# Issuing the first three up-weight loads from GpSimd's queue instead of SyncE's

## The chip, the cores and the metric

The kernel runs on one core of a Trainium2 chip. The metric is the device time of one execution in microseconds (us); lower is better. Before the change the median of three runs is 611.11 us (610.91 to 612.06).

## The reference

Two blocks run one after the other. The first is a linear attention with decay: 4 batches, 8 heads, 768 tokens, head size 64, worked in blocks of 64 tokens. Each block's output is its own masked scores times its values, plus its queries times a state that is carried from block to block:

```python
intra = einsum('bhic,bhjc->bhij', qb, kb) * Dmask[None]
intra = einsum('bhij,bhjd->bhid', intra, vb)
inter = einsum('bhid,bhde->bhie', qb * lam_pow[None], kv_state)
out[:, :, sl] = intra + inter
kv_state = lam_block * kv_state + einsum('bhsd,bhse->bhde', kb * rev_pow, vb)
```

Its output is laid out as `x`, 3072 tokens by 512 columns, and goes through a feed-forward block with a leaky ReLU:

```python
h = x @ w_in                    # (3072, 512) @ (512, 2048)
g = np.maximum(0.01 * h, h)
return (g @ w_out).astype(np.float32)
```

The weights `w_in` ("up") and `w_out` ("down") come as 64-bit floats, so one number of theirs is 8 bytes in memory.

## The kernel before, in words

**Attention.** The 3072 tokens are 24 chunks of 128 tokens (two blocks of 64 each). For chunk `c`, `load_kq` (L330) loads k and q in two halves of 128 KB each, and `load_v` (L374) loads v as one transfer of 256 KB. There are two buffers for each of k, q and v, used by turns, so that a load of chunk `c` has to wait until chunk `c - 2` has been read. TensorE transposes k and q (`transposes`, L391), ScalarE copies the transposes to SBUF (L402, L403), VectorE or GpSimd multiply in the decays (k at L407, q at L411), TensorE makes the scores and the product of k and v (`scores`, `quad` at L312), VectorE masks the scores (L440) and adds the product to the state (L445, L447), and GpSimd decays the state for the next block (L450). Then TensorE makes the output (L312 again), which ScalarE and VectorE split into three parts `xh`, `xl`, `xm` (L495, L496, L498) for an exact product in a faster number format.

**Up weights.** `w_in` is cut into 8 pairs of 128 columns. `w_in(p)` (L593) handles a pair in two halves `h`. For each half `to_float32` (L544) loads 512 KB of 64-bit floats into one of three `raw` buffers (L554), and turns them into 32-bit floats by three ScalarE instructions (L566, L568, L570) and two VectorE instructions (L572, L573). `parts` (L575) then splits the pair into `wh`, `wl`, `wm` (L579 or L581, L584, L590). The counter `n_raw` numbers these loads, and `raw[n_raw % 3]` is the buffer. The first three loads are both halves of pair 1 and the first half of pair 0.

**Products.** `up` (L616, matmuls at L628) multiplies a group of four chunks with a pair of weights and stores the result in DRAM; `down` (L676, matmuls at L688) reads it back and multiplies it with the down weights.

**Order.** All of this is written into a planner (`Plan`, L37). Each step has an engine and a planned cost; DMAs are on a lane of their own, called "DMA". `emit` runs a list schedule over these costs and issues the instructions in the planned order, so that each engine's queue has a fixed order. The plan also puts in idle transposes (`busy`, L262, L265) that keep TensorE running in gaps it foresees. Loads of q, k, v and weights are all issued from SyncE (SP). In the first 33 us SP's order is: k, q, v of chunks 0 and 1, weights (pair 1, first half), q and k of chunk 2, weights (pair 1, second half), v of chunk 2, q, k of chunk 3, q of chunk 4, v of chunk 3, weights (pair 0, first half), k of chunk 4, and so on.

A load needs its buffer free; beyond that, each DMA issued from SP takes one of eight completion semaphores by turns and waits for the DMA that had it before, eight DMAs earlier.

Of the kernel before, what the change touches and what calls it, by code (L numbers as in the profile page):

```python
# [36 lines left out]
class Plan:  # L37
# [23 lines left out]
    def add(self, eng, us, fn, reads=(), writes=(), rank=0.0):  # L61

        n, deps = len(self.ops), set()
        for k in reads:
            w, r = self.last.setdefault(k, [None, []])
            if w is not None:
                deps.add(w)
            r.append(n)
        for k in writes:
            w, r = self.last.setdefault(k, [None, []])  # L70
            if w is not None:
                deps.add(w)
            deps.update(r)
            self.last[k] = [n, []]
        deps.discard(n)
        ways = {eng: us} if isinstance(eng, str) else dict(zip(eng, us))
        if self.slack:
            self.more[n] = self.slack
        if self.chain is not None:
            self.chains[self.chain].append(n)  # L80
        self.ops.append((ways, fn, deps, (self.rank + rank, n), set(writes)))
# [81 lines left out]
def kernel(  # L163
# [10 lines left out]
    nc = tc.nc  # L174
# [34 lines left out]
    def sb(shape, name, dt=F32):  # L209
        return pool.tile(shape, dt, name=name, tag=name)  # L210
# [13 lines left out]
    raw = [sb([P, 2 * d_model], f"raw{i}") for i in range(NRAW)]  # L224
# [53 lines left out]
    def move(us, fn, reads, writes, issue=0.5, rank=0.0, slack=SLACK):  # L278

        plan.slack = slack if steady else EARLY_SLACK  # L280
        if steady and not rank:
            rank = FIRST
        add("DMA", length(us, issue), fn, reads, writes, rank=rank)
        plan.slack = 0.0
# [257 lines left out]
    n_raw = 0  # L542

    def to_float32(kind, p, h, dst, key, after=()):  # L544

        nonlocal n_raw
        j, n_raw = n_raw % (1 if kind == "wo" else len(raw)), n_raw + 1
        r, low, kl = raw[j], lows[n_raw % 2], f"low{n_raw % 2}"
        d = dst.bitcast(I32)

        def get():
            r64 = r.bitcast(I64)
            if kind == "wi":
                nc.sync.dma_start(out=r64.rearrange("p (k f) -> p k f", k=2),  # L554
                                  in_=w_in_r[:, 2 * h:2 * h + 2, p * 2 * P:(p + 1) * 2 * P])
            else:
                nc.sync.dma_start(out=r64, in_=moe_w_out[(2 * p + h) * P:(2 * p + h + 1) * P, :])

        def words(i, dt):
            return r.bitcast(dt).rearrange("p (n two) -> p n two", two=2)[:, :, i]  # L560

        def addend(dt, i):
            return low.bitcast(dt).rearrange("p (n two) -> p n two", two=2)[:, :, i]

        move(1.6, get, after, [f"raw{j}"])
        add("ACT", 0.67, lambda: nc.scalar.activation(out=dst, in_=words(1, F32), func=AF.Abs, scale=2.0 ** -110),  # L566
            [f"raw{j}"], [key])
        add("ACT", 0.78, lambda: nc.scalar.activation(out=addend(U16, 0), in_=words(0, U32), func=AF.Copy, bias=0.0, scale=2.0 ** -29),  # L568
            [f"raw{j}"], [kl])
        add("ACT", 0.77, lambda: nc.scalar.activation(out=addend(F16, 1), in_=words(1, F32), func=AF.Copy, bias=0.0, scale=2.0 ** -100),  # L570
            [f"raw{j}"], [kl])
        add("DVE", 0.42, lambda: nc.vector.tensor_scalar(d, d, 3, None, op0=ALU.logical_shift_left), [], [key])  # L572
        add("DVE", 1.0, lambda: nc.vector.tensor_tensor(d, d, low, op=ALU.add), [kl], [key])  # L573
# [19 lines left out]
    def w_in(p):  # L593
        for h in range(2):
            to_float32("wi", p, h, w32[:, h, :], f"w32{h}")
        parts(p, w32f, ["w320", "w321"])
# [5 lines left out]
    def w_out(p, h, after):  # L602
        to_float32("wo", p, h, w32[:, h, :], f"w32{h}", after)
        if h == 1:
            move(1.5, lambda: nc.sync.dma_start(out=WO[p], in_=w32f), ["w320", "w321"], [f"WO{p}"])
# [198 lines left out]
```

## Time and profile before

| what | value |
|---|---|
| median of three runs | 611.11 us |
| profiled execution, its own time | 611.72 us |
| its span, first to last instruction | 609.9 us |
| TensorE busy | 598.7 us, 98% of the span |
| VectorE / ScalarE / GpSimd busy | 312.6 / 270.3 / 83.2 us |
| DMA moved | 104.66 MB, mean 172 GB/s |
| granted TensorE clock | 0.999 |

The profile is of one execution. Busy time of an engine leaves out DMA-issuing instructions. In the timeline a line gives the start and the duration in us, the engine, the line of the kernel, what was written from what, how many instructions are merged (x4), and in brackets the idle time before, with what ended it. "SPq" is SP's own queue: the duration is how long SP was taken up with issuing. "Landing" is the time from the start of the issue until the completion was signalled.

### The profile page before, as it was taken

What the parts mean: (1) busy time and instruction counts of PE and PEld (TensorE: products, weight loads), DVE (VectorE), ACT (ScalarE), POOL (GpSimd) and SP (SyncE); (2) the same over time, 40 slices, a digit from 0 to 9 for tenths busy, and PEclk for the clock granted to TensorE, in tenths of its full rate; (3) what the DMA queues carried; (4) which work ended last, traced back from release to release, by engine and by line L of the source; (5) the groups of instructions that cost most, each with busy time, mean ns of one, the idle gap of its engine ahead of it and who ended that gap; (6) DMA issues with size and microseconds to landing.
All of it is one profiled execution on the core that took longest, in us unless ns stands there. A gap on an engine that the chain in (4) does not pass through costs nothing.

```text
span 609.9 us, 12921 instructions
## 1 busy us (share of the span) xinstructions
PE 598.7 (98%) x5402; PEld 496.0 (81%) x5402; DVE 312.6 (51%) x412; ACT 270.3 (44%) x434; POOL 83.2 (14%) x90
## 2 busy tenths in 40 slices
PE   7899999999999999999999999999999999999997
PEld 6678888888878888888888888888888888888886
DVE  5999980254253344335356745545454544635531
ACT  4678874444455656555576522222222313214111
POOL 1654400144142013113000000000000000000000
PEclk9999999999999999999999999999999999999999
DMA  9999976446799879976775943523434343433201
GB/s 211 225 261 257 267 197 163 132 112 158 166 219 267 209 201 244 248 225 182 291 248 207 287 158 103 173 70 139 138 103 133 111 136 108 134 103 124 84 1 69
DMA packets 141162, 104.66 MB, mean 172 GB/s; under 512 B 117040, under 2 KB 117808, under 8 KB 141104
## 3 DMA queue, kind: packets, MB, share of 16 engines
q1 hardware_dynamic: 140960, 103.83, 58.4%
q8 instruction: 42, 0.69, 0.5%
q14 instruction: 16, 0.13, 0.1%
q10 hardware_dynamic: 144, 0.00, 0.0%
HBM read 68.16 MB, written 35.65 MB: 170 GB/s over the span
## 4 chain that ended last, share of the span: by engine, by line
PE 94%; DVE 3%; DMA 1%; ACT 1%; SPq 0%; issue 0%; DVEq 0%
PE b L628 42%; PE b L688 18%; PE po L688 11%; PE psc L688 11%; PE psc L312 4%; PE po L312 4%; PE pt L688 4%; PE pt L391 1%; PE po L391 1%; DMA att<-in_k_dram 1%; DMA raw<-in_k_dram 0%; DVE att L440 0%; DVE att L411 0%; DVE att L447 0%; DVE w L572 0%; DVE wm L590 0%
## 5 line engine op out<-in xcount | busy, mean ns | idle before, releaser
L670 ACT ACTIVATE xh<-att 128x1024 fp32r<-128x1024 f32 x48 | 50.9, 1061 | 147.1 <-PE b L688 145.1
L671 DVE SCALAR_TENSOR_TENSOR xl<-att,xh 128x1024 fp32r<-128x1024 f32 x48 | 58.6, 1222 | 98.5 <-ACT xh L670 98.5
L628 PE MATMUL b<-xh,wh 128*128 128x512 f32 (+1 forms) x392 | 102.9, 386 | 0.8 <-ACT xh L495 0.8
L628 PE MATMUL b<-xm,wm 128*128 128x512 f32 (+1 forms) x392 | 103.2, 391 | 0.0
L628 PE MATMUL b<-xl,wl 128*128 128x512 f32 (+1 forms) x392 | 102.7, 386 | 0.0
L628 PEld LDWEIGHTS b<-xh,wh 128*128 128x128 f32 x392 | 72.6, 188 | 16.4 <-ACT xh L495 0.9
L628 PEld LDWEIGHTS b<-xl,wl 128*128 128x128 f32 x392 | 72.6, 188 | 14.8
L628 PEld LDWEIGHTS b<-xm,wm 128*128 128x128 f32 x392 | 71.2, 188 | 14.7
L649 ACT ACTIVATE gs<-b 128x512 f32<-128x512 f32 x96 | 57.0, 596 | 47.3 <-PE b L628 41.9
L646 ACT ACTIVATE b<-b 128x512 f32<-128x512 f32 x96 | 56.0, 584 | 49.5 <-PE b L628 49.3
L688 PE MATMUL b<-wh,xh 128*128 128x512 f32 x192 | 74.7, 389 | 0.0
L688 PE MATMUL b<-wl,xl 128*128 128x512 f32 x192 | 74.7, 389 | 0.0
L673 DVE SCALAR_TENSOR_TENSOR xm<-xl,xh 128x1024 fp32r<-128x1024 f32 x48 | 58.8, 1225 | 5.2 <-DVE xl L671 0.5
L440 DVE TENSOR_TENSOR att<-psc,att 128x512 f32<-128x512 f32 x24 | 16.5, 687 | 63.6 <-PE psc L312 63.4
L688 PEld LDWEIGHTS b<-wh,xh 128*128 128x128 f32 x192 | 36.1, 188 | 7.5
L688 PEld LDWEIGHTS b<-wl,xl 128*128 128x128 f32 x192 | 36.0, 188 | 7.5
L407 POOL TENSOR_TENSOR att<-att 128x512 f32<-128x512 f32 (+1 forms) x23 | 25.8, 1122 | 98.8 <-PE po L391 54.9
L450 POOL TENSOR_TENSOR att<-att 128x256 f32<-128x256 f32 x40 | 32.8, 821 | 44.5 <-DVE att L447 44.5
L572 DVE TENSOR_SCALAR w<-w 128x512 int32<-128x512 int32 x32 | 17.0, 530 | 40.8 <-ACT w L566 40.8
L688 PE MATMUL psc<-wh,xh 128*128 128x512 f32 x96 | 37.3, 389 | 0.0
L688 PE MATMUL psc<-wl,xl 128*128 128x512 f32 x96 | 37.3, 389 | 0.0
L688 PE MATMUL psc<-wm,xm 128*128 128x512 f32 x96 | 37.3, 389 | 0.0
(73 smaller groups left out, 809.7 us busy)
## 6 DMA issues: line engine op xcount, KB each, us to landing
att<-g SPq DMA_DIRECT2D x48, 512.0 KB, 3.3
g<-gs SPq DMA_DIRECT2D x47, 512.0 KB, 3.8
raw<-in_moe_w_in_dram SPq DMA_DIRECT2D x16, 512.0 KB, 5.7
raw<-in_moe_w_out_dram SPq DMA_DIRECT2D x16, 512.0 KB, 4.6
att<-in_k_dram SPq DMA_DIRECT2D x48, 128.0 KB, 4.3
att<-in_v_dram SPq DMA_DIRECT2D x24, 256.0 KB, 4.6
out_dram<-gs SPq DMA_DIRECT2D x23, 256.0 KB, 2.0
wo<-w SPq DMA_DIRECT2D x8, 512.0 KB, 5.2
```

The source lines that it names most:

```text
L312: nc.tensor.matmul(dst[HALF[cols]], lhsT=lhsT[HALF[rows]], rhs=rhs[HALF[rows]], start=start, stop=True, skip_group_check=True)
L407: lambda e="POOL": ENG[e].tensor_tensor(kr[nr], kr[nr], _bc(pow_k, 3, D)[nr], op=ALU.mult), ["fk"], [f"k{i}"])
L440: add("DVE", 0.69, lambda: nc.vector.tensor_tensor(sc, psc[:, :, lower, :], decay, op=ALU.mult), ["psc", "fk"], ["sc"])
L450: add("POOL", 0.7, lambda new=new, j=j: nc.gpsimd.tensor_tensor(state[(j + 1) % 4], new, _bc(lam_c, 2, D), op=ALU.mult), [f"st{j % 4}", "f ...
L572: add("DVE", 0.42, lambda: nc.vector.tensor_scalar(d, d, 3, None, op0=ALU.logical_shift_left), [], [key])
L628: nc.tensor.matmul(dst, lhsT=w[z][:, kk * 2 * P + f * P:kk * 2 * P + (f + 1) * P], rhs=x[z][:, kk, toks], start=start and kk == 0, stop=kk ...
L646: add("ACT", ns, lambda b=b: nc.scalar.activation(out=b, in_=b, func=AF.Copy, bias=0.0, scale=S + 1.0), [], [kb], rank=-1.5)
L649: add("ACT", ns, lambda b=b, r=r: nc.scalar.activation(out=r, in_=b, func=AF.Prelu, bias=0.0, scale=1.0 / WS, alpha=0.01), [kb], [f"gs{jg} ...
L670: add("ACT", 1.05, lambda: nc.scalar.activation(out=h, in_=graw[j], func=AF.Copy, bias=0.0, scale=NEAR), reads, wr("h"))
L671: add("DVE", 1.25, lambda: nc.vector.scalar_tensor_tensor(l, graw[j], 1.0, h.bitcast(F32), op0=ALU.mult, op1=ALU.subtract), reads + [f"rh{ ...
L673: add("DVE", 1.25, lambda: nc.vector.scalar_tensor_tensor(m, l.bitcast(F32), -S, h.bitcast(F32), op0=ALU.mult, op1=ALU.add), [f"rh{j}", f" ...
L688: nc.tensor.matmul(acc[tb][z // 2][:, cols], lhsT=ring[j][z][:, f * T + tb * P:f * T + (tb + 1) * P], rhs=W[pp][z][:, f * d_model:(f + 1) ...
```

## The change

The first three calls of `to_float32` (those in which `n_raw`, already counted up, is at most the number of `raw` buffers) issue their load from GpSimd's queue. Everything else is as before; the planner sees the same steps with the same costs, so the order on TensorE, VectorE and ScalarE stays as it was, SP's queue loses three entries, and GpSimd's queue gets three.

```diff
@@ -548,10 +548,13 @@
         r, low, kl = raw[j], lows[n_raw % 2], f"low{n_raw % 2}"
         d = dst.bitcast(I32)
 
+        first = n_raw <= len(raw)
+
         def get():
             r64 = r.bitcast(I64)
             if kind == "wi":
-                nc.sync.dma_start(out=r64.rearrange("p (k f) -> p k f", k=2),
+
+                (nc.gpsimd if first else nc.sync).dma_start(out=r64.rearrange("p (k f) -> p k f", k=2),
                                   in_=w_in_r[:, 2 * h:2 * h + 2, p * 2 * P:(p + 1) * 2 * P])
             else:
                 nc.sync.dma_start(out=r64, in_=moe_w_out[(2 * p + h) * P:(2 * p + h + 1) * P, :])
```

On GpSimd's queue the first load stands right after the start-up memsets (L268), ahead of the decay of k of chunk 1 (L407). The second stands right after that L407, ahead of the first decay of the state (L450). The third stands after the fourth L450, ahead of the fifth. None of the three waits for anything but its place in that queue, as the `raw` buffers are still unused.

## Prediction

> **What bounds the kernel now.** I read the page's busy times first, then the windows by stage.
>
> ```profile
> PE 598.7 (98%) x5402; PEld 496.0 (81%) x5402; DVE 312.6 (51%) x412; ACT 270.3 (44%) x434; POOL 83.2 (14%) x90
> ```
>
> ```profile
> 0.00:35.00 35.00, 28.39 (x613) 22.53 (x616) 25.75 (x52) 20.03 (x36) 15.17 (x22) 1.00 0.95 218
> 35.00:70.00 35.00, 35.00 (x550) 29.52 (x543) 32.92 (x44) 28.98 (x54) 16.68 (x13) 1.00 0.89 251
> ```
>
> The columns are the window, its length, then busy us of PE, PEld, DVE, ACT and POOL, the granted clock, the DMA share and GB/s. TensorE is without a gap from 35 us on; its idle time, 6.6 us of the 11.2 in all, lies in the first 35 us, and 3.8 more is the tail after its last matmul. So the change, whose loads all lie in the first 26 us, can only move the point at which TensorE's unbroken run begins. Whatever that start shifts by, the end shifts by. DMA is at 0.95 in the same window: issue slots are not all that is scarce there.
>
> Next, SP's timeline. It issues back to back from 0.74 us to 31 us, so each removed entry brings later ones forward:
>
> ```profile
> 1.78 1.06 SPq L337 DMA_DIRECT2D att<-in_q_dram  x2
> ...
> 6.73 1.12 SPq L554 DMA_DIRECT2D raw<-in_moe_w_in_dram  x1
> ...
> 10.29 1.92 SPq L554 DMA_DIRECT2D raw<-in_moe_w_in_dram  x1
> ...
> 15.19 2.87 SPq L337 DMA_DIRECT2D att<-in_k_dram  x2
> ...
> 19.25 0.46 SPq L376 DMA_DIRECT2D att<-in_v_dram  x1
> 19.75 0.57 SPq L554 DMA_DIRECT2D raw<-in_moe_w_in_dram  x1
> ```
>
> Then TensorE and VectorE where they wait for loads:
>
> ```profile
> 5.50 1.06 PE L391 MATMUL pt<-att 128*128 128x128 f32 x4
> ...
> 23.33 0.44 PE L391 MATMUL pt<-att 128*128 128x128 f32 x2 [0.45 <-DMA att<-in_q_dram]
> ...
> 24.49 1.16 PE L312 MATMUL psc<-att 64*64 64x64 f32 x64 [0.72 <-DVE xl L496]
> ...
> 25.71 0.69 DVE L440 TENSOR_TENSOR att<-psc,att 128x512 f32<-128x512 f32 x1 [1.35 <-PE psc L312]
> ```
>
> ```profile
> att<-in_q_dram SPq DMA_DIRECT2D x1, 128.0 KB, 3.4
> ...
> att<-in_v_dram SPq DMA_DIRECT2D x1, 256.0 KB, 5.1
> ```
>
> The first of these two lines is the second half of q of chunk 0 (issued 2.33 us, so landed at 5.7); the second is v of chunk 3, issued 19.25, landed 24.35. Two load waits sit on the path. The transposes of q of chunk 0 at 5.50 take 1.06 us, against 0.66 for the same four later: they wait for that half, with no slack. And the matmul at 24.49, put down to VectorE, starts right after v of chunk 3 landed; that is the real releaser. VectorE, busy without a real gap from 12.48 to 24.36, idles 1.35 us for it.
>
> **What the Trainium skill says.** "DMA: Bandwidth & Descriptors", section "Issuing engines are not separate DMA queues": DMAs of all issuers run on the same 16 engines, so another issuer saves only sequencer time. Its section "Queues, rings and completion order" adds that an engine goes round robin, a packet at a time, between queue rows that have work; no stretch here shows it, as nearly all bytes are on one queue (q1). Its section "Anatomy of one DMA — SWDGE (gpsimd) path" prices a DMA issued from GpSimd at 2.0 us plus bytes at 436 GB/s. "SBUF — State Buffer", section "SBUF: two separate sides", says that VectorE in a two-port mode keeps GpSimd from writing descriptors; no GpSimd DMA is in this trace to compare.
>
> **The change, part by part.**
>
> *SP loses 1.12 + 1.92 + 0.57 = 3.61 us of issuing.* Only part brings loads forward. The path load is v of chunk 3, behind k of chunk 3 (15.19), which overwrites k of chunk 1; TensorE reads that until 14.81. So k of chunk 3 can go at about 14.9 at best, 0.3 us earlier, however much SP is freed. The rest has to come from shorter issues in a shorter backlog: the second half of that k took 1.88 of the 2.87 us, against 0.45 for a short one, up to 1.4 us. If v and q of chunk 4 come in time, the product still waits for the decayed k (GpSimd L407 ends at 23.21), so L440 could begin at about 24.55: the most to win is 25.71 - 24.55 = 1.15 us. Range 0 to 1.15; I take 0.6, about half, since the third load, now on its own queue and begun at about 19.3 as before, can pass v of chunk 3, behind which it was queued until now.
>
> *The first load moves from 6.73 to about 1.35 us*, right after the memsets. It is now among the loads of chunk 0.
>
> ```profile
> q1 hardware_dynamic: 2048, 0.51, 49.3%
> ```
>
> ```profile
> 2.00:2.50 0.50, 0.50 (x5) 0.50 (x4) 0.00 (x0) 0.47 (x1) 0.00 (x0) 1.00 0.32 63
> ...
> 10.00:11.00 1.00, 0.88 (x40) 0.69 (x40) 0.59 (x2) 0.59 (x1) 0.83 (x1) 1.00 1.00 358
> ```
>
> The first is from the DMA view of 0 to 4.6 us: 0.51 MB has gone by, which is exactly k and q of chunk 0 (four times 128 KB). SP's first issue at 0.74 had its first packets just after 2.0, 1.3 us later. A GpSimd issue at 1.35 with the same lead gives 2.65; the page's fixed 2.0 us, much of which it puts after the data, gives at most 3.4 as an estimate. Both are before 4.6, so weights stand in front of q's data. In 10 to 11 us, when weights run alone, they go at 358 GB/s: 0.524 MB takes 1.46 us. Served with priority or packet by packet with 2 KB against 256 B, nearly all of it goes ahead: +1.4 us. Shared evenly or with fewer weights per turn, 0.4. Starting after 4.6: 0, since v (needed 8.80, landed 7.0), k and q of chunk 1 have 1.3 to 1.9 us in hand. I take +1.4. From q's transposes on, scores, L440 and the output follow in a fixed queue order, and VectorE after 12.48 has no gap to absorb it; so it passes in full to 24.36.
>
> *GpSimd issues three DMAs.*
>
> ```profile
> 10.17 1.06 POOL L407 TENSOR_TENSOR att<-att 128x512 f32<-128x512 f32 x1 [8.83 <-PE b L391]
> 11.19 0.62 POOL L450 TENSOR_TENSOR att<-att 128x256 f32<-128x256 f32 x1
> ...
> 18.29 1.00 POOL L450 TENSOR_TENSOR att<-att 128x256 f32<-128x256 f32 x1 [0.69 <-DVE att L447]
> ...
> 21.26 0.94 POOL L450 TENSOR_TENSOR att<-att 128x256 f32<-128x256 f32 x1 [1.96 <-DVE att L447]
> ```
>
> No such issue is in the trace. By SP's issues it holds its engine 0.4 to 1.9 us; I bound it at 0.4 to 2.5 and take 1.0. The first lies in 8.8 us of idle time: 0. The second goes between the first two lines; L447 on VectorE at 13.09 needs that L450, which ends at 11.81: 1.2 us of cover, so 0, and up to +1.3 at 2.5. The third lies in 1.96 us of idle time: 0, up to 0.5. A gain by holding GpSimd is excluded, as nothing is removed there.
>
> *Weights themselves.* The first is needed at 12.83, the second at 16.92 (GpSimd 11.2, plus the page's 2.0 + 1.2, is 14.4): neither is late. The third (now used at 25.89 after 0.55 us of waiting) comes earlier, but ScalarE's next path step, L495 at 28.49, waits for TensorE: 0.
>
> Sum: +1.4 - 0.6 + 0 = +0.8. Against the profiled execution (611.72 = 609.9 of span and 1.8 around it) that is 612.5; its time is 0.6 over the median of the runs, so against 611.11 I forecast 611.9.
>
> **Rivals.** *A late start on GpSimd* (faster): the first weights begin after 4.6 us and q of chunk 0 is untouched; only the earlier v of chunk 3 remains: -0.6 (0 to -1.15), 610.5. It decides if the first packet comes over 3.25 us after 1.35. Against it: the 1.3 us lead on SP.
> *GpSimd's hold is long* (slower by over 0.2%): an issue of over 1.2 us delays L450, then L447, then the product of chunk 1. At 2.0 us that is +0.8; and if the third load passes v of chunk 3, nothing is won there: 1.4 + 0.8 = +2.2 (1.3 to 3.2), 613.3. For it: the slow SP issues of 1.9 us; against it: the page's small price for descriptor generation.
> *It does nothing*: shared evenly, q loses 0.5, v of chunk 3 gains 0.5: 611.1.
>
> **Chances.** Forecast 0.45 (own range 611.1 to 612.7), late start 0.15, long hold 0.33, nothing 0.07. Over 0.2% is 1.2 us, about what a measurement tells from no change. Slower: nearly all of the long hold (0.31) and a fifth of the forecast (0.10), 0.41. Faster: a fifth of the late start, in which something is won beyond its own 1.15 us, 0.03. Same: 0.56. The range 610.5 to 613.5 leaves out about half of the late start and a third of the long hold, some 0.18.
>
> **What would show it.** Right: weights' packets before 4.6 us on a second queue, q's transposes at 5.50 stretched by about 1.4 us, L440 of chunk 0 at about 11 instead of 9.57, L440 of chunk 3 about 0.8 later than 25.71 with a shorter wait than 1.35, and the first unbroken L628 run shifted by as much. Wrong: L440 of chunk 0 still at 9.57; a POOL gap of over 1.2 us ahead of L450; or a shift that arises after 35 us, where I see no room.

## The result and the profile after

| what | before | after |
|---|---|---|
| median of the runs compared (10 each) | 611.59 us (610.87 to 614.28) | 614.59 us (613.6 to 615.33) |
| ratio, 95% interval | | 1.0035 (1.0021 to 1.0049) |
| profiled execution, its own time | 611.72 us | 614.6 us |
| its span | 609.9 us | 612.8 us |

In what follows, "before" and "after" are short for the two kernels. By the ratio the change costs 2.1 us (0.0035 of 611.6; 1.3 to 3.0 by its interval); the two medians lie 3.0 us apart. Taken a second time (run e9 below) it is 613.69 against 611.45, a ratio of 1.0042 (1.0029 to 1.0055). The forecast of 611.9 us and its range up to 613.5 were too low.

First the page of after: the busy line, and two of the DMA queues.

```profile
PE 599.3 (98%) x5402; PEld 495.9 (81%) x5402; DVE 314.0 (51%) x412; ACT 270.2 (44%) x434; POOL 85.5 (14%) x93
...
q1 hardware_dynamic: 140144, 102.26, 56.9%
q0 software_dynamic: 432, 1.57, 0.7%
```

TensorE does the same work. A new queue, q0, carries the three loads: 1.57 MB in 432 packets, 3.6 KB each, against 0.7 KB on q1. GpSimd's 93 instructions and 85.5 us take in its three DMA issues (90 and 83.2 before), unlike the issues of SP. VectorE is 1.4 us busier than before with the same 412 instructions: keep that in mind. Next the two windows that answer to those of before (columns as there).

```profile
0.00:35.00 35.00, 27.27 (x583) 21.23 (x584) 24.38 (x50) 18.74 (x33) 16.88 (x24) 1.00 0.88 210
35.00:70.00 35.00, 34.39 (x556) 29.12 (x555) 33.13 (x44) 28.79 (x53) 17.06 (x14) 1.00 0.87 250
```

TensorE lost 1.1 us in the first window (28.39 before), and it now has 0.61 us of idle time in the second, where it had none. So there is a loss at the start, as forecast, and one later, which was not. The issues of GpSimd and of SP:

```profile
1.48 0.87 POOL L557 DMA_DIRECT2D raw<-in_moe_w_in_dram  x1
...
13.89 0.74 POOL L557 DMA_DIRECT2D raw<-in_moe_w_in_dram  x1
...
21.96 0.74 POOL L557 DMA_DIRECT2D raw<-in_moe_w_in_dram  x1
```

```profile
3.44 4.01 SPq L337 DMA_DIRECT2D att<-in_k_dram  x2
...
20.74 0.46 SPq L376 DMA_DIRECT2D att<-in_v_dram  x1
```

GpSimd is held 0.74 to 0.87 us by each. SP, which was to gain time, pays at once: the two issues of k of chunk 1 take 4.01 us, against 1.45 before. v of chunk 3 is issued at 20.74 (19.25 before) and lands 3.60 us later, at 24.34, as early as before. Then TensorE and VectorE at the places named in the prediction:

```profile
7.78 1.17 PE L391 MATMUL pt<-att 128*128 128x128 f32 x4 [2.22 <-DMA att<-in_q_dram]
...
25.98 1.16 PE L312 MATMUL psc<-att 64*64 64x64 f32 x64 [0.17 <-POOL att L407]
```

```profile
12.28 0.69 DVE L440 TENSOR_TENSOR att<-psc,att 128x512 f32<-128x512 f32 x1 [2.25 <-PE psc L312]
...
27.21 0.69 DVE L440 TENSOR_TENSOR att<-psc,att 128x512 f32<-128x512 f32 x1
```

The transposes of q of chunk 0 wait 2.22 us for q, and L440 of chunk 0 comes 2.71 us later than before (9.57). At chunk 3 the wait for v is gone (1.35 us before) and L440 is 1.50 us later (25.71 before): 1.2 of the 2.7 us are won back. v itself is no earlier than before; the later start uses up the wait for it, until the decayed k (GpSimd L407) ends the wait instead. From there on the shift of the same TensorE instruction against before is followed in a table; it was found by laying the two traces side by side, instruction by instruction.

| place in the kernel before | shift of after | what happened there |
|---|---|---|
| 25.7 us, L440 of chunk 3 | +1.5 | start: 2.7 lost, 1.2 won |
| 42.9 us, L312 into `po` | +1.04 | before waits some 0.3 us each for ScalarE (38.8 us) and for k of chunk 6, after doesn't |
| 50.0 us, L628 | +1.94 | VectorE and GpSimd in each other's way |
| 165.5 us, L628 | +3.0 | a gap of 0.76 us for which the trace shows no wait |
| 176.0 us, scores | +3.06 | nothing much up to the end: TensorE ends at +3.1, the span is +2.9 |

**The step at 43 to 47 us.** The timeline of before and then of after, VectorE and GpSimd alone, with the conversion of weights on VectorE (L572 and L581 of before are L575 and L584 of after):

```profile
42.42 0.42 DVE L572 TENSOR_SCALAR w<-w 128x512 int32<-128x512 int32 x1
42.66 1.10 POOL L407 TENSOR_TENSOR att<-att 128x512 f32<-128x512 f32 x1 [1.16 <-PE po L391]
42.98 1.33 DVE L573 CUSTOM_DVE_ANT_0 w<-w,low 128x1024 uint16<-128x1024 uint16 x1
44.34 0.69 DVE L581 TENSOR_SCALAR wh<-w 128x1024 fp32r<-128x1024 f32 x1
...
45.12 0.74 POOL L411 TENSOR_TENSOR att<-att 128x256 f32<-128x256 f32 x1 [1.37 <-PE po L312]
```

```profile
43.70 1.34 POOL L407 TENSOR_TENSOR att<-att 128x512 f32<-128x512 f32 x1 [0.58 <-PE po L391]
...
44.04 1.28 DVE L575 TENSOR_SCALAR w<-w 128x512 int32<-128x512 int32 x1
...
46.17 0.74 POOL L411 TENSOR_TENSOR att<-att 128x256 f32<-128x256 f32 x1 [1.13 <-PE po L312]
46.19 1.27 DVE L584 TENSOR_SCALAR wh<-w 128x1024 fp32r<-128x1024 f32 x1
...
49.57 0.73 PE L631 MATMUL b<-xl,wl 128*128 128x512 f32 x2 [0.61 <-DVE wl L587]
```

A tensor_scalar has one tensor as input, a tensor_tensor two. In before VectorE's instruction begins first each time and takes 0.42 and 0.69 us. In after GpSimd begins first, by 0.34 and 0.02 us, and the same two instructions take 1.28 and 1.27 us, +1.44 together. Before pays 0.64 us of it elsewhere (its L573 at 42.98 takes 1.33 us instead of 0.69), which leaves 0.8. VectorE then delivers `wl` late, and TensorE waits 0.61 us for it at 49.57. In before VectorE led by 0.24 us. In after TensorE, which releases GpSimd's L407, has made up 0.58 us on VectorE, and so GpSimd leads. About half of that is the wait for k of chunk 6, which before has and after has not; the other half is a wait for ScalarE (L649) at 38.8 us in before. TensorE's transposes of k of chunk 6, in before (where the weight loads for them wait 0.3 and 0.2 us for k) and in after:

```profile
41.68 0.84 PE L391 MATMUL po<-att 128*128 128x128 f32 x4
```

```profile
42.96 0.60 PE L391 MATMUL po<-att 128*128 128x128 f32 x4
```

The Trainium skill has the stretching in "SBUF — State Buffer", section "Who interferes with whom": VectorE in a two-port mode, which a tensor_scalar can take, and GpSimd use one shared pair of ports, and the first to begin holds it for its whole instruction. The trace agrees: the instruction that takes 0.42 us in before ends in after 0.28 us behind GpSimd's of 1.34 us (45.32 and 45.04). That VectorE is in this mode here no run shows.

**The gap at 165 us** is read last, with the runs that show it.

### The profile page after: what moved, and what is told of

It is laid out like the page before. It is cut to its first block, busy times and chain, and to the rows that moved or that the text cites. A ratio compares the mean times of both kernels' runs of the same rounds, so it can differ in the third digit from the quotient of the medians.

```text
span 612.8 us, 12922 instructions
## 1 busy us (share of the span) xinstructions
PE 599.3 (98%) x5402; PEld 495.9 (81%) x5402; DVE 314.0 (51%) x412; ACT 270.2 (44%) x434; POOL 85.5 (14%) x93
## 3 DMA queue, kind: packets, MB, share of 16 engines
q0 software_dynamic: 432, 1.57, 0.7%
## 4 chain that ended last, share of the span: by engine, by line
PE 91%; DVE 5%; DMA 1%; SPq 1%; POOL 1%; issue 1%; ACT 0%; DVEq 0%; POOLq 0%
PE b L631 40%; PE b L691 18%; PE po L691 11%; PE psc L691 11%; PE pt L691 4%; PE po L312 3%; PE psc L312 3%; DMA att<-in_q_dram 1%; DVE w L575 1%; PE pt L391 1%; DVE w L576 1%; SPq L363 1%; DVE wm L593 1%; SPq L337 0%; DVE att L447 0%
## 5 line engine op out<-in xcount | busy, mean ns | idle before, releaser
L649 ACT ACTIVATE b<-b 128x512 f32<-128x512 f32 x96 | 56.0, 585 | 51.0 <-PE b L631 50.8
L440 DVE TENSOR_TENSOR att<-psc,att 128x512 f32<-128x512 f32 x24 | 16.5, 687 | 60.9 <-PE psc L312 60.6
L407 POOL TENSOR_TENSOR att<-att 128x512 f32<-128x512 f32 (+1 forms) x23 | 26.0, 1131 | 102.2 <-PE po L391 55.2
L450 POOL TENSOR_TENSOR att<-att 128x256 f32<-128x256 f32 x40 | 33.0, 825 | 41.9 <-DVE att L447 40.8
L575 DVE TENSOR_SCALAR w<-w 128x512 int32<-128x512 int32 x32 | 17.5, 546 | 40.4 <-ACT w L569 40.4
```

The costliest lines, as they stand in the source:

```text
L407: lambda e="POOL": ENG[e].tensor_tensor(kr[nr], kr[nr], _bc(pow_k, 3, D)[nr], op=ALU.mult), ["fk"], [f"k{i}"])
L440: add("DVE", 0.69, lambda: nc.vector.tensor_tensor(sc, psc[:, :, lower, :], decay, op=ALU.mult), ["psc", "fk"], ["sc"])
L450: add("POOL", 0.7, lambda new=new, j=j: nc.gpsimd.tensor_tensor(state[(j + 1) % 4], new, _bc(lam_c, 2, D), op=ALU.mult), [f"st{j % 4}", "f ...
L649: add("ACT", ns, lambda b=b: nc.scalar.activation(out=b, in_=b, func=AF.Copy, bias=0.0, scale=S + 1.0), [], [kb], rank=-1.5)
```

## The experiments

Times are medians; "before" is measured on the same chip with each set, 611.44 to 611.65 us in the sets where the medians are given below. Shifts are of one profiled execution against the profiled execution of before. Tenths of a microsecond at L440 of chunk 0 are not to be read: in the six other profiles with nothing issued ahead of q of chunk 0 (e2, e4, e6, e8, e10, e11) it begins at 9.10 to 10.36 us, although q lands at 5.67 to 5.94. Theory A, ahead of all runs: the loss is made at the start, by the first load's bytes going ahead of q of chunk 0. The rival: it is made by the second and third load, or by GpSimd as the issuer.

### One part of the change at a time

Only the first load from GpSimd (`first = n_raw == 1`):

> Only the first of the three loads goes from GpSimd; the second and third stay on SP. Theory A (the first load's data stand in front of q of chunk 0, and the other two cost nothing): q of chunk 0 lands at about 8.2 us as in the changed kernel (5.7 before), L440 of chunk 0 begins at about 12.3, and the time is 2 to 3.5 us over the kernel before. Theory B (issuing from GpSimd costs by itself, each load a part): about a third of the loss, 1 us.

Measured: 614.84 (613.87 to 615.41), ratio 1.0046 (1.0032 to 1.0059): all of the loss and, if anything, more. L440 of chunk 0 is at 12.98, +3.4 us, and at chunk 3 still +2.6 (v of chunk 3 lands at 25.64 here).

Only the second and third from GpSimd (`first = 1 < n_raw <= len(raw)`):

> The second and third load go from GpSimd, the first stays on SP at its old place. Theory A: q of chunk 0 lands at 5.7, L440 of chunk 0 is back at 9.6, v of chunk 3 comes earlier, so the time is at or below the kernel before, 0 to -1.2 us. Theory B: about two thirds of the loss, 1.5 to 2 us over the kernel before.

Measured: 612.3, ratio 1.0013 (1.0002 to 1.0024). The gain that Theory A wants did not come. The start is untouched (L440 of chunk 0 at 9.10), but TensorE then waits twice. From its timeline:

```profile
23.85 0.44 PE L391 MATMUL pt<-att 128*128 128x128 f32 x2 [1.13 <-DMA att<-in_q_dram]
...
25.79 1.16 PE L312 MATMUL psc<-att 64*64 64x64 f32 x64 [1.50 <-DMA att<-in_v_dram]
```

Here the third load, issued at 18.83, goes beside q of chunk 4 (from 18.25) and ahead of v of chunk 3 (19.36), and v lands at 25.65 instead of 24.35. That is the passing that the prediction feared. In after it doesn't happen: there the late start put the third load (21.96) behind v (20.74). So the first load makes the loss. With it gone a smaller one is left: in the profile TensorE is 1.3 us late at chunk 3, where v is late beside the third load, and it loses 0.9 us more at 47.6 us, with both tensor_scalars stretched as in after.

### Bytes, issuer or queue

The first load as early as in after, but from ScalarE's queue; the other two from SP:

```diff
     nc.scalar.dma_start(out=lam_b, in_=lam.partition_broadcast(P))
+    nc.scalar.dma_start(out=raw[0].bitcast(I64).rearrange("p (k f) -> p k f", k=2),
+                        in_=moe_w_in.rearrange("(ko ki) n -> ki ko n", ki=P)[:, 0:2, 2 * P:4 * P])
...
```

Further down, `get` leaves out the first load on SP.

> The first load is issued at the same early time (about 1.2 us), but from ScalarE's queue, and the other two from SP. Theory A in its plain form (only the early bytes count, 0.52 MB at 358 GB/s): q of chunk 0 is late by 1.4 to 2.5 us whoever issues, time 1 to 3 us over the kernel before. Theory B, or a cost that is particular to how GpSimd's loads are served: q of chunk 0 late by 0.5 us at most, time within 0.6 us of the kernel before.

Measured: 613.0, ratio 1.0021 (1.0012 to 1.003). L440 of chunk 0 is 2.45 us late, of chunk 3 1.28. So early bytes delay q whoever issues them. But the issuer, or what goes with it, counts too: the same single load costs a ratio of 1.0021 from ScalarE and 1.0046 from GpSimd (e1, same set), and the two intervals don't meet. In the profiles e1 is 1.3 us further behind at chunk 3, and it has the step at 47.6 us and the gap at 165 us, which e3 has not. The two loads differ in their packets and in how evenly their parts end; no run separates these. The DMA queues in 3.9 to 5.5 us, first in after, then in this run (packets, MB, share):

```profile
q0 software_dynamic: 108, 0.42, 74.7%
q1 hardware_dynamic: 298, 0.08, 20.7%
```

```profile
q10 hardware_dynamic: 198, 0.37, 62.9%
q1 hardware_dynamic: 666, 0.17, 46.3%
```

In before q1 moved 0.40 MB in 1596 packets in that time. With the weights beside it, q1 is down to 0.08 MB in after and to 0.17 here. By bytes the weights win, as their packets are large: 3.9 KB in the mean (0.42 MB by 108) and 1.9 KB against 256 B. The Trainium skill's "DMA: Bandwidth & Descriptors", section "Queues, rings and completion order", has each DMA engine go round robin between queues, a packet at a time. A queue of small packets falling behind one of large ones fits that. The counts here are about 3 small ones for each large; but the section's packet is a group of descriptors, typically 9 to 17, and how the profile's packets relate to those no run shows.

Only half of the first load early (256 KB from GpSimd, the other half from SP at the old place; the other loads from SP):

```diff
...
+                for z in range(2) if first else ():
+                    (nc.sync if z else nc.gpsimd).dma_start(out=r64.rearrange("p (k f) -> p k f", k=2)[:, z, :],
+                                                            in_=w_in_r[:, 2 * h + z, p * 2 * P:(p + 1) * 2 * P])
...
```

> The first load is cut in two: 256 KB from GpSimd at the early place, the other 256 KB from SP at the old place; the second and third load from SP. If the loss at the start is the weights' bytes in front of q of chunk 0, half the bytes delay it by about half: q lands at about 7 us instead of 8.2 to 8.5, L440 of chunk 0 at about 11, and the time is about 1.5 us over the kernel before. If the loss is a fixed price of a GpSimd issue (first use, descriptors), q lands at 8.2 or later all the same.

Measured: 612.16, ratio 1.0005 (0.9996 to 1.0013), not told from before. The second half of q lands at 6.78, 1.03 us late against 2.46 in after; L440 of chunk 0 is 1.30 us late (in a stretch, 9 to 11 us, in which the granted TensorE clock was 0.50, so that q is the better measure) and of chunk 3 0.30. Half the bytes cost about half the delay, which a fixed price of GpSimd's issue would not. The 1.5 us that were expected in the time did not come: 1.0 of the 1.3 us are gone by chunk 3.

### The first load held until q has landed

GpSimd copies two columns of q of chunk 0 ahead of the first load, and so waits for it:

```diff
...
+                if number == 1:
+                    nc.gpsimd.tensor_copy(hold, kqv[1][0][:, 0:2 * HP:HP, 0])
...
```

> All three loads go from GpSimd as in the changed kernel, but a copy of two columns of q of chunk 0 on GpSimd stands ahead of the first, so that it is issued only when q has landed (about 5.8 us). Theory A: q of chunk 0 at 5.7, L440 of chunk 0 near 9.6, and the time 0 to -1.2 us against the kernel before. Theory B: three issues from GpSimd as before, so the loss stays, 2 to 3 us.

> The first load from GpSimd, held until q of chunk 0 has landed, the second from GpSimd, the third on SP again, behind v of chunk 3. If the third load from GpSimd gets in front of q of chunk 4 and v of chunk 3 (as it did with the first on SP: v landed at 25.65), v of chunk 3 now lands at 22 to 23 and L440 of chunk 3 begins at 24.6 to 25; the time is then 0 to 1 us under the kernel before, unless what follows at 43 us takes it back (0.85 us). If loads from GpSimd cost wherever they stand, it is 1 us or more over.

Measured: with all three from GpSimd (e4) 613.02, ratio 1.0022 (1.0012 to 1.0032); with the third back on SP (e6) 611.47, ratio 1.0003 (0.9994 to 1.0013). In e4 the start is as before (L440 of chunk 0 at 9.54), v of chunk 3 lands at 22.30, and TensorE's product for it begins 0.8 us ahead of before. Theory A wants a gain, and the median shows a loss of 1.3 to 1.6 us against before. So A is not all of it. Three later places lose what was won: a gap of 1.03 us at 25.6 us, the step of 0.94 us at 47.6 us with both tensor_scalars stretched (1.28 and 1.26 us), and 0.8 us at 165 us. e6 shows all three too, in a profiled run that was its slowest (613.67); its v of chunk 3 lands at 22.57, as expected, but L440 of chunk 3 begins at 26.16, behind the gap at 25 us.

### The step at 43 to 47 us

The changed kernel with twelve small memsets on GpSimd ahead of the decay of k of chunk 6, so that L407 comes after VectorE's conversion:

```diff
...
+            def decay_k(e="POOL"):
+                for _ in range(12 if c == 6 else 0):
+                    nc.gpsimd.memset(pause, 0.0)
+                ENG[e].tensor_tensor(kr[nr], kr[nr], _bc(pow_k, 3, D)[nr], op=ALU.mult)
...
```

It was run twice, the second time in one set with the changed kernel itself (e9):

> The changed kernel with twelve small memsets on GpSimd ahead of the decay of k of chunk 6, so that it starts about 0.4 to 1.4 us later. If the second part of the loss is this decay running into VectorE's shift and split of the weights at 43 to 47 us (1.28 instead of 0.42 us, 1.27 instead of 0.69), those are short again, TensorE stays about 1.1 us behind the kernel before at 50 us instead of 2.0, and the time is 0.5 to 0.9 us under the changed kernel. If that stretch is no part of the loss, the time stays at the changed kernel's, about 3 us over.

> The changed kernel with twelve small memsets on GpSimd ahead of the decay of k of chunk 6, beside the changed kernel in the same set. If the collision is what the changed kernel loses at 43 to 47 us: 0.8 us under it in the median, about 613.8, and 0.42 and about 0.7 for the two tensor_scalars. If the time is not made or lost there (the difference found earlier was between two sets of runs): no difference, 614.6.

> The changed kernel itself, once more, beside the other three of this set. Theory A (two places: the start, and the collision of GpSimd with VectorE at 43 to 47 us): about 614.6 in the median, 3.0 over before; in the profile the tensor_scalar at about 44 us again takes 1.28 us and the one at about 46 us 1.27, L440 of chunk 0 comes at about 12.3. Whether TensorE's gap at 165 us is part of the change: if it is, it is there again; if it comes from run to run, the chance is about even that it is not. Rival (the collision is a chance of the one profiled run): 0.42 and 0.69, and a TensorE shift of +1.1 to +1.3 from 43 us on.

Measured: e7 613.81, ratio 1.0031 (1.0019 to 1.0043); e12 613.8, ratio 1.004 (1.0028 to 1.0052); e9 613.69, ratio 1.0042 (1.0029 to 1.0055). From the timeline of e12, in which L582 and L591 are the two conversions and L411 is GpSimd's decay of k:

```profile
45.16 0.42 DVE L582 TENSOR_SCALAR w<-w 128x512 int32<-128x512 int32 x1
...
46.45 0.74 DVE L591 TENSOR_SCALAR wh<-w 128x1024 fp32r<-128x1024 f32 x1
46.82 1.28 POOL L411 TENSOR_TENSOR att<-att 128x512 f32<-128x512 f32 x1
```

The collision is gone, and with it TensorE's step at 47.6 us. Over all profiled runs this has no exception (times are those of before):

| runs | two tensor_scalars, us | TensorE's step from 47.5 to 50 us |
|---|---|---|
| after, e1, e2, e4, e6, e9 | 1.28 or 1.29 and 1.23 to 1.28 | +0.91 to +0.94 |
| e3 | 1.28 and 0.69 | +0.05 |
| before, e5, e7, e8, e10, e11, e12 | 0.42 and 0.69 to 0.74 | 0.00 |

Wherever GpSimd's tensor_tensor began first (in e1 once at the same 0.01 us), VectorE's instruction was stretched; wherever VectorE began first, it was not. e3, a single profile, says that it is the second of the two that costs TensorE time. But the medians of e12 and e9 are the same: the pause did not show as a gain there. In the profiles both are at +2.5 us at 26.5 us. e12 then waits for k of chunk 6 again (its transposes take 0.84 us) and is at +2.4 at 43 us, where e9 is at +1.9; the pause spares it the step, so that at 50 us it is 0.4 us ahead (+2.4 and +2.8); and it has the gap at 165 us (0.9 us), which e9 has not. So the place is shown by the traces, and that a kernel gets faster by removing it is not shown by the times.

Two more with the pause, the kernel before and the held kernel e6:

> The kernel before with nothing but the twelve memsets. It has a smaller collision of its own: VectorE's custom instruction at 42.98 us takes 1.33 us instead of 0.69 beside GpSimd's decay of k. If such overlaps cost what they show: up to 0.6 us less than before, 611.0 to 611.4 beside 611.6, as the moved GpSimd work may run into the next instruction instead (0.3 us there in the changed kernel with the pause). If the pause as such costs or gives time apart from the collision, it shows here: slower by 0.5 or more would mean the decayed k comes late.

> The first load from GpSimd but held until q of chunk 0 has landed, the second from GpSimd at once, the third from SP, and the twelve memsets ahead of the decay of k of chunk 6. Held and third on SP alone it was 611.5 with 1.28 and 1.23 us for the two tensor_scalars. If the collision is worth what it shows, 0.8 to 0.9 less: 610.7, and 0.3 to 0.9 us below before. If TensorE's path does not go through these two instructions there, no change: 611.5. If the pause delays the decayed k for chunk 6 so that its product is late: 612 to 613.

Measured: before with the pause (e11) 611.44 against 611.45, ratio 0.9999 (0.9989 to 1.0009). Its own 0.64 us of overlap is gone (0.69 instead of 1.33), and TensorE gets nothing from it, so VectorE had that much room there; that the pause as such costs anything doesn't show. e10 is 611.0, ratio 0.9991 (0.9979 to 1.0004): the lowest median of all, but its interval still includes 1. From its timeline on TensorE and on VectorE:

```profile
23.55 1.48 PE L313 MATMUL psc<-att 64*64 64x64 f32 x64 [0.17 <-POOL att L411]
```

```profile
9.85 0.69 DVE L446 TENSOR_TENSOR att<-psc,att 128x512 f32<-128x512 f32 x1 [2.21 <-PE psc L313]
...
25.10 0.69 DVE L446 TENSOR_TENSOR att<-psc,att 128x512 f32<-128x512 f32 x1 [0.45 <-PE psc L313]
```

In this profile, this is what two freed issue slots are worth when nothing is put in front of q: the product of chunk 3 is 0.9 us earlier than before (24.49), and L440 of it 0.6 (25.71), as a stop of 0.3 us at 25 us lies between.

### Gaps for which no wait is shown

The kernel before was run once more:

> The kernel before once more, for a second profile. If its first profile is typical, q of chunk 0 lands at 5.7, v of chunk 3 near 24.4, the VectorE instructions at 42.4 and 44.3 take 0.42 and 0.69 us, and TensorE has no gap near 165 us. If what the profiles show after 40 us is chance, some of these differ.

Measured: 611.24 us, span 609.5. It has the wait for v of chunk 3 put down to v itself, which confirms how the prediction read that wait:

```profile
24.37 1.16 PE L312 MATMUL psc<-att 64*64 64x64 f32 x64 [0.94 <-DMA att<-in_v_dram]
```

It also lacks a stop that the first profile of before has ahead of the scores at 176.04 us, worth 0.7 us of TensorE; after has it as well, and most other runs don't. So single stops of this size differ between two runs of one kernel. The stops at two other places are put down to "issue", always at the same points of TensorE's instruction stream: near 25 us (after 47 matmuls of L312) and near 165 us. In the timelines of after and of e9:

```profile
167.86 1.21 PE L631 MATMUL b<-xl,wl 128*128 128x512 f32 x4 [0.76 <-issue]
```

```profile
27.69 0.46 PE L312 MATMUL psc<-att 64*64 64x64 f32 x17 [0.75 <-issue]
```

"issue" says that TensorE waited for nothing that the profile shows. What goes with them is queue q8, "instruction", one packet of 16 KB at a time. The eighteenth such packet starts at 160.1 us in before. With TensorE's shift at that point taken off, it starts at most 0.3 us later in e2, e3, e5, e7 to e11 (nine profiles with before), none of which has the gap at 165 us; and 3.4 to 3.8 us later in after, e1, e4, e6 and e12, all of which have it (0.8 to 1.3 us of TensorE). The third packet, near 21 us, goes the same way with the gap at 25 us, though less far apart: against TensorE's shift just ahead of that gap it is 1.7 to 3.0 us late in e4, e6, e9, e10 and e12, which have it (0.3 to 1.3 us), and at most 1.4 in the rest. Of these only e11 loses time there, for another reason: its granted TensorE clock was 0.58 from 24 to 26 us. The ends of the packets say the same. In each of the five stops at 165 us TensorE goes on 1.2 to 1.4 us after the packet has ended, and in each of the five at 25 us 1.5 to 1.6 us after; without a stop it came to these points no sooner than 2.2 and 1.5 us after the packet's end. That program code arriving late starves TensorE is the reading that fits; no run here made the packet late on purpose. Whether the change makes it likelier is open. The gap at 165 us is in after and not in e9, which are the same kernel. It is in 5 of the 9 profiles that take the first load from GpSimd, and in none of the 5 others.

## Why the prediction was wrong

**What holds.** The bound and the mechanism: TensorE's unbroken run begins later, as the first load's bytes go ahead of q of chunk 0 (e1, e3 and e5 show it). GpSimd's holding cost nothing: 0.87 and 0.74 us against the 1.0 assumed, under the covers of 8.8, 1.2 and 1.96 us, and L440 is 2.7 us late at chunks 0, 1 and 2 alike. The wait at 24.49 was for v of chunk 3 (e8 names it), and v comes in time in the changed kernel.

**The term +1.4 was too small.** The second half of q landed 2.46 us later (8.21 instead of 5.75), and L440 of chunk 0 came at 12.28, not "at about 11". The load is complete when the slowest of its 16 parts is, and the forecast reckoned with one rate for all. Of the 16 completions of that half of q, in order of time, the first thirteen came 1.2 to 1.6 us later than before (the first at 6.31 instead of 4.76), which is about what was forecast; the last three came 2.0 to 2.6 us later. The weights' own completions spread from 5.70 to 7.71 us, so some engines were done with them 2 us before others. From ScalarE (e3) q's completions spread from 6.82 to 7.69 us, no wider than before, and all were 1.6 to 2.1 us late. That is nearer to what the rate gives: 358 GB/s was that of weights alone; mixed with q and k, from 3.5 to 6 us, the five half microseconds of e3 show 321, 356, 353, 304 and 285 GB/s, a mean of 324, by which 0.524 MB take 1.6 us (an estimate). Why the parts end so unevenly from GpSimd is open.

**The term -0.6 was too small as well.** 1.2 us were won back by chunk 3. That is the 1.15 which the prediction gave as the most to win, and for the reason it gave: the product then waits for the decayed k, as after's line at 25.98 says. It took half, as it thought that the third load could pass v; that happened only in e2. The errors of the two terms partly cancel: with both as measured the sum is +1.5 instead of +0.8, and the forecast 612.6.

**The step that failed** is that nothing arises after the start: "whatever that start shifts by, the end shifts by", and in the last sentence "a shift that arises after 35 us, where I see no room". The sum has no term for it. In after TensorE's shift is +1.5 at chunk 3 and +3.1 at the end; in e9, the same kernel, +1.5 and +2.05. The ground for it was misread too. "Without a gap from 35 us on" was taken from a window that ends at 70 us; the prediction's own numbers leave 0.8 us of idle time over (11.2 - 6.6 - 3.8), and in before they are a stop of 0.28 us at 295 us and this one, behind a load of k that VectorE had waited for:

```profile
176.04 0.69 PE L312 MATMUL psc<-att 64*64 64x64 f32 x32 [0.48 <-DVE att L371]
```

And TensorE being without a gap from 35 to 70 us shows that its partners were in time, not that they had room. At 43 us the order of VectorE and GpSimd hung on 0.24 us; after it had turned, the collision cost 0.9 us of TensorE in the traces. Nothing in the window's busy sums tells of it: they show 35.00 of 35.00. What each of the late places is worth in the median stays open: the kernel without the collision was no faster (e12 613.8, e9 613.69), and the gaps at 25 and 165 us are in some profiles of one kernel and not in others.

**The sum of after, as measured** in its profile: 2.7 - 1.2 = +1.5 at chunk 3, -0.5 by 42.9 us, +0.9 by the collision, +1.1 at 165 us and 0.1 later, +3.1 for TensorE; the tail after its last matmul is 0.2 us shorter, which gives the span's +2.9. The term of 165 us is not in every run (e9: span +1.8, with 1.0 at 25 us instead, and without the 0.7 that before has at 176 us).

**The rivals.** The long hold on GpSimd forecast 613.3 and came nearest in time, for a wrong reason: GpSimd was held 0.74 to 0.87 us, not over 1.2. The late start did not happen: the weights' first packets came at 3.58 us, before 4.6. Of "it does nothing", nothing is left.

## What to carry to other kernels

Moving a load to another queue does not only save issue time: it takes the load out of its place in line, so look first at whose bytes it will be beside, and at the packet sizes of both. A delay at the start does not pass through unchanged; two engines that get in each other's way can swap order by tenths of a microsecond, so look for pairs whose starts lie that close, even where the bounding engine is full, and add up the idle time that a busy window leaves out. And where a forecast is under 1 us in 600, take the profile of the same kernel twice before a single gap in it is explained.

## What the runs showed of the hardware

- A DMA of 512 KB issued from GpSimd held it 0.74 to 0.87 us. The first packets of the first load came 2.1 us after its issue began in after (1.48 to 3.58), and 1.7 to 2.7 us in the other runs. The three of after took 6.2, 5.2 and 5.7 us to land.
- Beside a queue with packets of 3.9 KB, a queue with packets of 256 B fell from 0.40 to 0.08 MB in 1.6 us.
- At 43 to 47 us, VectorE's tensor_scalar of 0.42 us took 1.28 or 1.29 us, and one of 0.69 us 1.23 to 1.28 us, whenever GpSimd's tensor_tensor had begun first, by as little as 0.02 us.
- TensorE stood still for 0.3 to 1.3 us at two fixed points of its instruction stream in those profiles in which a packet of the queue "instruction" came over 1.6 us late, and went on 1.2 to 1.6 us after the packet's end.
